# First transform of k times v crossed with the last quarter of the paired inverse; an arena part of its own, load tiles that share buffers

## The chip, the cores and the metric

The kernel runs on one core of one Trainium2 chip. The metric is device time in microseconds, from one launch of the program; every number called "us" is of that kind or a time inside one profiled execution. A difference between two kernels is given as a ratio of times.

A core has five engines with their own instruction streams. TensorE (PE) multiplies matrices and writes to PSUM, which has eight banks. ScalarE (ACT) and VectorE (DVE) read PSUM and SBUF. GpSimd (POOL) does little here. The sync engine (SP) issues nearly all DMA transfers, in one queue and in order. Engines wait for each other through semaphores.

## The reference

Inputs have S = 2048 rows and D = 1024 channels; the MLP has F = 3584. The kernel computes the output and the gradients of ten inputs (bf16).

```
xn   = layernorm(x)
ksh  = sum over t of shift(k, t) * shift_k[:, 3 - t]      # 4 taps along the sequence
kv   = ksh * v
y    = irfft(rfft(kv, 2S) * rfft(ssm_k, 2S))[:S] + kv * ssm_D
h    = relu(xn @ W_gate) * (xn @ W_up)
out  = x + xn * y + h @ W_down
```

The gradients with respect to x, k, v, shift_k, ssm_k, ssm_D, W_gate, W_up and W_down follow from it. For the long convolution that means three forward transforms per channel (ssm_k, the gated gradient g = grad_out * xn, and kv), products of spectra, and inverse transforms for y, for the gradient of ssm_k (gh) and for the gradient of kv (gkv).

## The kernel before

Two parts are woven together. `LnMlp` does layer norm and the MLP forward and backward: nearly all its work is 128x512 matmuls with a contraction over 128 rows, called big matmuls here. `ABranch` does the long convolution, in 8 groups of 128 channels, as small matmuls in corners of the array (32x64 or 64x32 pieces), evictions by ScalarE, transposes and products by VectorE.

`LnMlp` runs in phases. `hidden` makes gate, up and the gradient of h for a block of 512 columns of F at a time. For each row tile: 8 matmuls into ps_g, a ReLU on ScalarE (L1143), 8 into ps_u, a mask (L1150) and a product (L1156) on VectorE and a store; 8 into ps_h, an eviction on ScalarE (L1278), one product of the gradient with both halves of ru on VectorE (L1279) and a store of ug_d. The last rows of a block are marked `hold`. `grad_down` and `grad_in` make the gradients of the weights by `gemm16` and, at three places, by `four`, which keeps four accumulators, so four PSUM banks, at a time. `out_phase` and `grad_x` come last, after the branch has ended. I count big matmuls from the start of the program; `hidden` ends at 2765, and `four` covers 2765 to 2829 and 3597 to 3725.

The branch is a generator, `slots`: each item is one slot with a TensorE part (or None) and a VectorE part. `steps` (L575) takes the next slot when the MLP has issued enough matmuls: 1900 ns of them in the hidden phase, later 1900 after a slot with a TensorE part and 1250 after one without. A slot thus lies at a fixed place among the big matmuls. With `pri.strict` set, every engine keeps this program order.

Loads are queued by `fetch`. `steps` issues one queued load per slot, but none while `hold` is set; `need` issues what is queued up to a load that is about to be used. SP then takes them in its own order.

A group's steady course, with the names that the profile shows:

- The second forward transform of g and k·v (FW, `f2_pair`) reads two transposed tiles (`flp`) that VectorE made by `flip` (L332, two STREAM_TRANSPOSE for each tile).
- Spectral products on VectorE (`cmul`, `turn`: 128x2048 and 128x1024 tensor_tensor, recorded at L91).
- The first inverse of gkv (IA, `inv_a`), its first steps crossed with the next group's filter (`hn`); transposes; second inverse (RB, `inv_b`) with evictions at L87; gks and gv; their stores and the halo copies of gks.
- The paired first inverse of y and gh (`inv_a_pair`), four quarters of 32 matmuls each. Two are crossed with the first transform of the next group's g (`gt`), after `gate_grad` has multiplied gt by `xt`.
- The taps of the gradient of k (`tg`), flips, the y step (RB with a piece of the second filter transform), flips, the gh step.
- In between, the taps of the next group's k (`tk` into `ksh`), the product `kvt` = ksh * vt, its first transform (two steps of 8 matmuls, 512 columns wide), and flips of g and k·v for the next group.

All PSUM tiles, of both parts, come from one pool of eight banks. `crossed` (L495) takes two rounds each of an inverse and of a forward transform on different row quarters of the array and issues them alternately by `joint` as one step. Each of the four jobs of a forward round takes a bank, and so does each of an inverse's.

The tiles of the branch lie in pools: `lng` (ksh, kp, vt), `ld` (hn, gt), `a_xt` (xt), `ts` (three tiles for kvt, gks, gv, gk, yt, gh, gkv), and the arena of eight parts of 4096 columns, where the spectra and the row forms of g, k·v and the inverses (`Bg`, `Bk`, `Cs`, `Cy`, `Ch`) share parts. Part 6 holds `Bk` and also half of `Cs`, so the first transform of k·v cannot be written before the inverse's `Cs` has been transposed.

## Time and profile before

| what | us |
|---|---|
| median of 3 runs | 1860.21 (1859.41 to 1860.25) |
| profiled run | 1859.57 |
| span in it | 1857.8 |
| TensorE busy | 1836.3 (99%) |
| VectorE busy | 1114.7 (60%) |
| ScalarE busy | 646.0 (35%) |
| VectorE busy, 117 to 690 (branch and hidden phase) | 451.8 of 573 |
| VectorE busy, 690 to 1240 (branch and weight gradients) | 364.6 of 550 |

A line of a timeline gives start, duration, engine, line, operation, out<-in, tile and how many instructions were joined; in square brackets the idle time before it and what ended that. TensorE's granted clock is 1.000 throughout. Matmuls overlap: a big matmul lasts 0.38 us and the next begins 0.216 us after its start. The end of a matmul is modelled.

### The profile page before, as it was taken

Reading aid. Unit: us, or ns where it says so; the run is one execution under the profiler, and the core shown is the slowest. Engines: PE = TensorE matmul, PEld = TensorE weight load, DVE = VectorE, ACT = ScalarE, POOL = GpSimd, SP = SyncE. Lnnn points to the kernel's source line nnn. Section 1 sums busy time; section 2 is a strip of 40 time slices with the busy share of each in tenths; the row PEclk is TensorE's granted clock in tenths of the full one; section 3 lists DMA queues with packets and bytes.
Section 4 is the critical chain, followed back from the end, with each engine's and each line's share of the span. In section 5 each row is a group of like instructions: output and inputs, shape, how many; then the busy total and the mean of one; then the engine's idle time right before and its main releaser. Section 6 shows DMA issues by size and latency. Waiting matters only on the chain.

```text
span 1857.8 us, 31871 instructions
## 1 busy us (share of the span) xinstructions
PE 1836.3 (99%) x12840; PEld 844.2 (45%) x13061; DVE 1114.7 (60%) x1635; ACT 646.0 (35%) x1215; POOL 19.2 (1%) x51
## 2 busy tenths in 40 slices
PE   9999999999999999999999999999999999999999
PEld 4444444444444444444444444444444544444444
DVE  6656888798698777685585874801222222466652
ACT  5645444444545445544545454320000000111100
POOL 1000000000000000000000000000000000000000
PEclk9999999999999999999999999999999999999999
DMA  9898499779559838368474363488999857799973
GB/s 266 246 238 184 130 226 226 191 172 208 151 145 242 251 91 213 118 159 259 120 184 132 110 183 110 136 222 235 252 243 254 184 141 166 177 210 213 206 151 74
DMA packets 748132, 344.65 MB, mean 186 GB/s; under 512 B 576088, under 2 KB 715344, under 8 KB 747984
## 3 DMA queue, kind: packets, MB, share of 16 engines
q1 hardware_dynamic: 736848, 320.31, 71.2%
q10 hardware_dynamic: 9504, 17.04, 2.9%
q0 software_dynamic: 1632, 5.24, 0.8%
q8 instruction: 102, 1.67, 0.4%
q14 instruction: 46, 0.38, 0.1%
HBM read 143.79 MB, written 103.83 MB: 133 GB/s over the span
## 4 chain that ended last, share of the span: by engine, by line
PE 97%; issue 1%; DVE 1%; DMA 1%; ACT 0%; SPq 0%; DVEq 0%; ACTq 0%
PE ps_x L1666 21%; PE ps_w L1370 20%; PE ps_h L1035 10%; PE ps_g L1035 10%; PE ps_u L1035 10%; PE ps_o L1534 10%; PE ps_d L1370 9%; PE ps_c L83 4%; PE ps_d L1386 1%; PE ps_w L1386 1%; PE ps_r L1568 0%; DMA wu<-in_B_W_up_dram 0%; PE pst_x L1074 0%; DMA ugs<-ug_d 0%; DMA ln_x<-in_A_q_dram 0%
## 5 line engine op out<-in xcount | busy, mean ns | idle before, releaser
L1370 PE MATMUL ps_w<-ugs,xn_nat 128*128 128x512 bf16 x1673 | 376.0, 379 | 4.4 <-issue 2.4
L87 ACT CAST arena<-ps_c 128x512 bf16<-128x512 f32 x576 | 294.7, 609 | 76.5 <-PE ps_c L83 76.2
L1035 PEld LDWEIGHTS <-xnT 128*128 128x128 bf16 x1792 | 171.6, 98 | 210.7 <-issue 8.2
L332 DVE STREAM_TRANSPOSE arena<-arena 128x1024 f32<-128x1024 f32 x96 | 179.9, 1934 | 128.1 <-ACT arena L87 109.8
L1370 PEld LDWEIGHTS <-xn_nat 128*128 128x128 bf16 x1728 | 165.0, 98 | 201.8 <-issue 8.1
L1035 PE MATMUL ps_u<-wu,xnT 128*128 128x512 bf16 x873 | 205.0, 379 | 1.7 <-DMA wu<-in_B_W_up_dram 0.2
L1035 PE MATMUL ps_g<-wg,xnT 128*128 128x512 bf16 x871 | 204.4, 379 | 2.0 <-DVE xnT L1079 0.3
L1035 PE MATMUL ps_h<-wdT,goT 128*128 128x512 bf16 x867 | 203.0, 379 | 2.3 <-DVE ru L1150 0.7
L1666 PE MATMUL ps_x<-wgT,ggT 128*128 128x512 bf16 x879 | 197.5, 379 | 0.9
L1666 PE MATMUL ps_x<-wuT,guT 128*128 128x512 bf16 x877 | 197.4, 379 | 1.0
L1684 ACT ACTIVATE w<-xn,m 128x512 f32<-128x512 bf16 x32 | 24.3, 806 | 479.9 <-DVE m L1677 366.6
L1534 PE MATMUL ps_o<-wd,hT 128*128 128x512 bf16 (+1 forms) x878 | 186.6, 372 | 0.9
L1370 PE MATMUL ps_d<-g_nat,hs 128*128 128x512 bf16 x740 | 167.9, 379 | 1.9 <-issue 0.8
L1666 PEld LDWEIGHTS <-guT 128*128 128x128 bf16 x896 | 87.7, 98 | 105.7
L1666 PEld LDWEIGHTS <-ggT 128*128 128x128 bf16 x896 | 87.7, 98 | 105.5
L1278 ACT CAST gh<-ps_h 128x512 bf16<-128x512 f32 x112 | 66.4, 593 | 195.1 <-PE ps_h L1035 188.4
L1035 PEld LDWEIGHTS <-goT 128*128 128x128 bf16 x896 | 86.2, 98 | 104.3 <-issue 2.5
L1534 PEld LDWEIGHTS <-hT 128*128 128x128 bf16 x896 | 87.7, 98 | 99.9
L1373 ACT CAST wi<-ps_w 128x512 bf16<-128x512 f32 x108 | 64.4, 596 | 190.0 <-PE ps_w L1370 158.9
L1526 DVE TENSOR_TENSOR ya<-ya,xe 128x1024 bf16<-128x1024 bf16 x16 | 11.1, 693 | 185.0 <-DMA xe<-xn_d 185.0
L1150 DVE SCALAR_TENSOR_TENSOR ru<-ru,ps_u 128x512 bf16<-128x512 bf16 x112 | 76.4, 682 | 66.0 <-PE ps_u L1035 41.7
L91 DVE TENSOR_TENSOR t<-arena 128x2048 bf16<-128x2048 bf16 x96 | 113.8, 1219 | 0.5
(145 smaller groups left out, 1378.8 us busy)
## 6 DMA issues: line engine op xcount, KB each, us to landing
ugs<-ug_d SPq DMA_DIRECT2D x112, 256.0 KB
ug_d<-ru SPq DMA_DIRECT2D x110, 256.0 KB
wg<-in_B_W_gate_dram SPq DMA_DIRECT2D x56, 256.0 KB
wu<-in_B_W_up_dram SPq DMA_DIRECT2D x56, 256.0 KB
hs<-h_d SPq DMA_DIRECT2D x56, 256.0 KB
out_dram<-wi SPq DMA_DIRECT2D x56, 256.0 KB
h_d<-ht SPq DMA_DIRECT2D x108, 128.0 KB
gt<-in_grad_out_dram SPq DMA_DIRECT2D x32, 256.0 KB
```

Of the source, the lines that this page charges most:

```text
L83: self.pri.pin(self.nc.tensor.matmul(out, lhsT=lhsT, rhs=rhs, start=start, stop=stop))
L87: self.pri.pin(self.nc.scalar.copy(out=out, in_=in_))
L91: self.pri.pin(self.nc.vector.tensor_tensor(out=out, in0=in0, in1=in1, op=op))
L332: self.pri.pin(self.nc.vector.transpose(out=df[:, c0:c0 + 32, :], in_=sf[:, c0:c0 + 32, :]))
L1035: self.pri.pin(self.nc.tensor.matmul(ps[:], lhsT=xT[:, kt * P:(kt + 1) * P], rhs=w(kt), start=(kt == 0), stop=(kt == self.DT - 1)), always ...
L1150: return self.pri.pin(nc.vector.scalar_tensor_tensor(out=ru[s][:, 1, :], in0=ru[s][:, 0, :], scalar=0.0, in1=ps[:], op0=ALU.is_gt, op1=ALU ...
L1278: self.pri.pin(nc.scalar.copy(out=gh[:], in_=ps[:]))
L1370: self.pri.pin(self.nc.tensor.matmul(ps[:], lhsT=lhsT(st), rhs=rhs(st), start=(st == 0), stop=(st == self.ST - 1)))
L1373: self.pri.pin(self.nc.scalar.copy(out=out, in_=ps[:]))
L1386: self.pri.pin(self.nc.tensor.matmul(ps[i][:], lhsT=lhsT(i, st), rhs=rhs(i, st), start=(st == 0), stop=(st == self.ST - 1)))
L1534: nc.tensor.matmul(ps, lhsT=hT[:, kt, :], rhs=self.wd[:, kt, oc], start=(kt == 0), stop=(kt == self.FT - 1))
L1666: nc.tensor.matmul(ps, lhsT=T[:, kt, :], rhs=W[:, kt, oc], start=(i == 0), stop=(i == n - 1))
```

## The change

Crossing: `crossed` now takes the quarter's number k and returns just two steps. The paired inverse's quarter 0 is crossed with g as before, and its quarter 3 with the first transform of k·v of the next group. For this, `Bk` has its own ninth arena part, and ksh, kvt and the taps of the next group are made ahead of the end of the inverse, in the slots where gk's taps were; the gk taps move behind and round the crossing.

Buffers: hn and kp share one buffer (tag "hk"), xt and ksh share one ("kx"), the pool `a_xt` is gone, and kvt is written over kp. A load into a shared buffer waits for the last reader of the tile before. So xt is fetched after the stores of gv, just ahead of its use, k and its taps after the crossing with the filter, and the filter of the group after next after the k·v crossing.

Slots: the two flips of y, the y step, the two flips of h, the gh step, and the four flips of k·v and g follow each other without tap slots between. A steady group has 73 slots instead of 76, 16 with a TensorE part instead of 17. The first group is reordered likewise: the gate product in its first slot, then the filter and g, then k.

```diff
-        arena = self.pool("a_are", 1, side="right").tile([P, 8, NB1 * P], BF16, name="arena")
+        arena = self.pool("a_are", 1, side="right").tile([P, 9, NB1 * P], BF16, name="arena")
-        self.Bg, self.Bk, self.H, self.GKV = rows(7), rows(6), spectrum(4), spectrum(7)
+        self.Bg, self.Bk, self.H, self.GKV = rows(7), rows(8), spectrum(4), spectrum(7)
...
-        st["hn"] = self.ld.tile([P, 2, 32, NB1], BF16, name="hn")
+        hn = self.lng.tile([P, 19, P], BF16, name="hn", tag="hk")[:, 0:16, :].rearrange("p r c -> p (r c)")
...
-        xt = st["xt"] = self.xp.tile([P, 16, P], BF16, name="xt")
+        xt = st["xt"] = self.lng.tile([P, 16, P], BF16, name="xt", tag="kx")
...
-    def crossed(self, inv, fwd):
-        I, F = inv[0], fwd[0]
-        return [self.joint(I[0][0:1], I[1][0:1], F[2], F[3]), self.joint(F[0], F[1], I[2][0:1], I[3][0:1])] + inv[1][1:]
+    def crossed(self, I, F, k):
+        I = [g[k:k + 1] for g in I]
+        return [self.joint(I[0], I[1], F[2], F[3]), self.joint(F[0], F[1], I[2], I[3])]
...
     def start_kvt(self, st):
-        kvt = st["kvt"] = self.ttile("kvt")
-        self.tt(kvt[:, 0:16, :], st["ksh"][:], st["vt"][:], ALU.mult)
+        st["kvt"] = st["kp"][:, 0:16, :]
+        self.tt(st["kvt"], st["ksh"][:], st["vt"][:], ALU.mult)
...
         self.store_time(self.out_gv, st["cg"], gv)
+        self.fetch(nx, self.load_xn)
         yield [], lambda: self.halo(st)
-        self.fetch(nx, self.load_k, self.load_taps)
-        ia = self.inv_a_pair()
+        ia, inv = self.inv_a_pair()
+        q = self.cmul(K, G, True, G, 1)
+        yield inv[1], q
+        for _ in range(4):
+            yield None, q
+        q = self.cmul(H, K, False, K, 1)
         if last:
-            ia = [ia[1][0], None] + ia[1][1:]
+            cross = [inv[0], None]
         else:
             self.need(self.load_xn, nx)
             yield None, lambda: self.gate_grad(nx)
-            self.fetch(n2, self.load_xn)
-            ia = self.crossed(ia, self.fwd1(self.Bg, nx["gt"]))
...
+            cross = self.crossed(ia, self.fwd1(self.Bg, nx["gt"])[0], 0)
+        yield None, q
+        yield cross[0], q
         yield None, q
         yield None, q
...
+        yield cross[1], q
         self.fetch(n2, self.load_g)
+        f2H, cross = [], [inv[3], None]
+        if not last:
+            f2H = [(1, self.f2(H, 1, j)) for j in range(4)]
+            self.need(self.load_k, nx)
+            self.need(self.load_taps, nx)
+            self.begin(nx)
+            tk = nx["tk"]
+            yield None, tk
+            yield None, tk
+            yield inv[2], tk
+            yield None, tk
+            yield f2H[0:2], tk
+            yield None, tk
+            yield None, tk
+            self.need(self.load_v, nx)
+            yield None, lambda: self.start_kvt(nx)
+            cross = self.crossed(ia, self.fwd1(self.Bk, nx["kvt"])[0], 3)
...
+        yield cross[0], tg
         yield None, tg
         yield None, tg
...
+        yield cross[1], tg
+        self.fetch(n2, self.load_filter)
+        if not last:
+            yield None, tg
+            yield None, tg
         self.store_time(self.out_gk, st["cg"], gk)
         fly = self.flip_C(self.Cy, 0)
         yield None, fly
         yield None, fly
-        tk = None
-        if not last:
-            self.need(self.load_k, nx)
-            self.need(self.load_taps, nx)
-            self.begin(nx)
-            tk = nx["tk"]
-        yield None, tk
-        yield None, tk
-        yield f2H[2:3] + self.inv_b(st, "yt", 0), tk
+        yield f2H[2:3] + self.inv_b(st, "yt", 0), None
+        yield None, None
         self.store_time(self.y_d, st["cg"], st["yt"])
         flh = self.flip_C(self.Ch, 0)
         yield None, flh
         yield None, flh
-        yield None, tk
-        yield None, tk
-        yield f2H[3:4] + self.inv_b(st, "gh", 0), tk
-        yield None, tk
-        yield None, None
+        yield f2H[3:4] + self.inv_b(st, "gh", 0), None
...
-        yield None, lambda: self.start_kvt(nx)
-        f1k = self.fwd1(self.Bk, nx["kvt"])[1]
-        yield None, lambda: self.store_gh(st)
-        flG = self.flip_B(self.Bg, 0)
-        yield f1k[0], None
-        yield None, flG
-        yield f1k[1], flG
-        yield None, None
         flK = self.flip_B(self.Bk, 1)
         yield None, flK
         yield None, flK
+        flG = self.flip_B(self.Bg, 0)
+        yield None, self.both(lambda: self.store_gh(st), flG)
+        yield None, flG
         yield None, None
-        yield None, None
```

More of the change, by code (lines that the diff above doesn't have):

```diff
@@ L115, in open @@
         self.tmp = self.pool("a_tmp", 2, side=R)
-        self.xp = self.pool("a_xt", 1, side=R)
         self.sm = self.pool("a_sm", 2, side=R)
@@ L270, in load_filter @@
     def load_filter(self, st):
-        st["hn"] = self.ld.tile([P, 2, 32, NB1], BF16, name="hn")
+        hn = self.lng.tile([P, 19, P], BF16, name="hn", tag="hk")[:, 0:16, :].rearrange("p r c -> p (r c)")
+        st["hn"] = hn.rearrange("p (h c n) -> p h c n", h=2, n=NB1)
         self.load_rows(st, 0)
@@ L297, in load_k @@
         nc = self.nc
-        kp = st["kp"] = self.lng.tile([P, 19, P], BF16, name="kp")
+        kp = st["kp"] = self.lng.tile([P, 19, P], BF16, name="kp", tag="hk")
         self.pri.now()
@@ L588, in steps @@
         yield 3400
-        self.load_k(st)
-        self.load_taps(st)
-        yield 3400
         self.load_g(st)
@@ L594, in steps @@
         self.load_v(st)
+        yield 3400
+        self.load_taps(st)
         yield 6800
@@ L599, in steps @@
         self.open_arena()
-        self.begin(st)
         for st in self.sts:
@@ L613, in begin @@
     def begin(self, st):
-        st["ksh"] = self.lng.tile([P, 16, P], BF16, name="ksh")
+        st["ksh"] = self.lng.tile([P, 16, P], BF16, name="ksh", tag="kx")
         st["tk"] = self.taps(st, st["ksh"], st["kp"], [(3, 0), (2, 1), (1, 2), (0, 3)])
     def start_kvt(self, st):
-        kvt = st["kvt"] = self.ttile("kvt")
-        self.tt(kvt[:, 0:16, :], st["ksh"][:], st["vt"][:], ALU.mult)
+        st["kvt"] = st["kp"][:, 0:16, :]
+        self.tt(st["kvt"], st["ksh"][:], st["vt"][:], ALU.mult)
     def flip_H(self):
@@ L639, in first @@
     def first(self, st):
-        tk, f1h, nx = st["tk"], self.fwd1_filter(st)[1], self.ahead(st, 1)
-        yield f1h[0], None
-        yield None, tk
-        yield f1h[1], tk
-        self.fetch(nx, self.load_filter)
-        yield None, self.both(lambda: self.add_D(st), tk)
-        yield None, tk
+        f1h, nx = self.fwd1_filter(st)[1], self.ahead(st, 1)
+        yield f1h[0], lambda: self.gate_grad(st)
+        yield None, None
+        yield f1h[1], None
+        self.load_k(st)
+        f1g = self.fwd1(self.Bg, st["gt"])[1]
+        yield None, lambda: self.add_D(st)
         flH = self.flip_H()
+        yield f1g[0], flH
         yield None, flH
-        yield None, flH
-        yield None, tk
-        yield None, tk
-        f2H = [(1, self.f2(self.H, 1, j)) for j in range(4)]
-        yield f2H[0:2], lambda: self.gate_grad(st)
-        self.fetch(nx, self.load_xn)
-        yield None, tk
-        yield f2H[2:4], lambda: self.start_kvt(st)
-        yield None, None
-        f1g, f1k = self.fwd1(self.Bg, st["gt"])[1], self.fwd1(self.Bk, st["kvt"])[1]
-        yield f1g[0], None
-        yield None, None
         yield f1g[1], None
         self.fetch(nx, self.load_g)
+        f2H = [(1, self.f2(self.H, 1, j)) for j in range(4)]
+        yield None, None
+        flG = self.flip_B(self.Bg, 0)
+        yield f2H[0:2], flG
+        yield None, flG
+        self.begin(st)
+        tk = st["tk"]
+        yield None, tk
+        yield f2H[2:4], tk
+        for _ in range(5):
+            yield None, tk
+        yield None, lambda: self.start_kvt(st)
+        f1k = self.fwd1(self.Bk, st["kvt"])[1]
         yield None, None
         yield f1k[0], None
-        flG = self.flip_B(self.Bg, 0)
-        yield None, flG
-        yield f1k[1], flG
+        yield None, None
+        yield f1k[1], None
+        self.fetch(nx, self.load_filter)
         yield None, None
@@ L707, in slots @@
             self.need(self.load_rest, nx)
-            iaG = self.crossed(iaG, self.fwd1_filter(nx))
+            iaG = self.crossed(iaG[0], self.fwd1_filter(nx)[0], 0) + iaG[1][1:]
         yield iaG[0], q
@@ L713, in slots @@
         yield None, lambda: self.turn(H, 1, 1)
-        self.fetch(n2, self.load_filter)
+        self.fetch(nx, self.load_k, self.load_taps)
         q = self.cmul(K, G, True, G, 0)
@@ L750, in slots @@
             yield None, lambda: self.gate_grad(nx)
-            self.fetch(n2, self.load_xn)
-            ia = self.crossed(ia, self.fwd1(self.Bg, nx["gt"]))
-        yield None, None
-        q = self.cmul(K, G, True, G, 1)
-        yield ia[0], q
+            cross = self.crossed(ia, self.fwd1(self.Bg, nx["gt"])[0], 0)
+        yield None, q
+        yield cross[0], q
         yield None, q
         yield None, q
-        yield ia[1], q
-        yield None, q
-        q = self.cmul(H, K, False, K, 1)
+        yield cross[1], q
         self.fetch(n2, self.load_g)
-        yield None, q
-        yield ia[2], q
-        yield None, q
-        yield None, q
-        yield None, q
-        gk = self.ttile("gk")
-        tg = self.taps(st, gk, gks, [(0, 0), (1, 1), (2, 2), (3, 3)])
+        gk = self.ttile("gk") if last else None
+        tg = self.taps(st, gk, gks, self.TAPS) if last else None
+        f2H, cross = [], [inv[3], None]
[10 more added lines that the diff above has]
+            yield f2H[0:2], tk
+            yield None, tk
+            yield None, tk
+            self.need(self.load_v, nx)
+            yield None, lambda: self.start_kvt(nx)
+            cross = self.crossed(ia, self.fwd1(self.Bk, nx["kvt"])[0], 3)
+            gk = self.ttile("gk")
+            tg = self.taps(st, gk, gks, self.TAPS)
+        else:
+            yield inv[2], tg
+            yield None, tg
+        yield None, tg
+        yield cross[0], tg
         yield None, tg
         yield None, tg
-        yield ia[3], tg
-        yield None, tg
-        yield ia[4], tg
-        yield None, tg
-        f2H = [] if last else [(1, self.f2(H, 1, j)) for j in range(4)]
-        yield f2H[0:2], tg
+        yield cross[1], tg
+        self.fetch(n2, self.load_filter)
+        if not last:
+            yield None, tg
+            yield None, tg
         self.store_time(self.out_gk, st["cg"], gk)
@@ L780, in slots @@
         yield None, fly
-        tk = None
-        if not last:
-            self.need(self.load_k, nx)
-            self.need(self.load_taps, nx)
-            self.begin(nx)
-            tk = nx["tk"]
-        yield None, tk
-        yield None, tk
-        yield f2H[2:3] + self.inv_b(st, "yt", 0), tk
+        yield f2H[2:3] + self.inv_b(st, "yt", 0), None
+        yield None, None
         self.store_time(self.y_d, st["cg"], st["yt"])
@@ L793, in slots @@
         yield None, flh
-        yield None, tk
-        yield None, tk
-        yield f2H[3:4] + self.inv_b(st, "gh", 0), tk
-        yield None, tk
-        yield None, None
+        yield f2H[3:4] + self.inv_b(st, "gh", 0), None
         if last:
+            yield None, None
             yield None, lambda: self.store_gh(st)
             return
-        self.need(self.load_v, nx)
-        yield None, lambda: self.start_kvt(nx)
-        f1k = self.fwd1(self.Bk, nx["kvt"])[1]
-        yield None, lambda: self.store_gh(st)
-        flG = self.flip_B(self.Bg, 0)
-        yield f1k[0], None
-        yield None, flG
-        yield f1k[1], flG
-        yield None, None
         flK = self.flip_B(self.Bk, 1)
@@ L813, in slots @@
         yield None, flK
+        flG = self.flip_B(self.Bg, 0)
+        yield None, self.both(lambda: self.store_gh(st), flG)
+        yield None, flG
         yield None, None
-        yield None, None
+    TAPS = [(0, 0), (1, 1), (2, 2), (3, 3)]
 A_START = 60_000
```

## The prediction

> **What bounds the kernel now.** I read first the busy shares, then the chain of waits by engine, then the timelines of TensorE, VectorE, ScalarE and the sync engine's queue round the steps that move.

> ```profile
> PE 1836.3 (99%) x12840; PEld 844.2 (45%) x13061; DVE 1114.7 (60%) x1635; ACT 646.0 (35%) x1215; POOL 19.2 (1%) x51
> PE   9999999999999999999999999999999999999999
> DVE  6656888798698777685585874801222222466652
> PE 97%; issue 1%; DVE 1%; DMA 1%; ACT 0%; SPq 0%; DVEq 0%; ACTq 0%
> ```

> TensorE is the bound in all forty slices (granted clock 1.000). VectorE is at 0.8 to 0.9 in the first third, the hidden phase, where its queue also holds the MLP's masks and products. So the change can gain only TensorE time, and can lose whatever it makes TensorE wait.

> What a branch step costs TensorE, from its timeline:

> ```profile
> 1059.64 7.29 PE L1370 MATMUL ps_w<-ugs,xn_nat 128*128 128x512 bf16 x32
> 1066.86 0.30 PE L83 MATMUL ps_c<-arena,IA 32*64 32x256 bf16 x4
> ...
> 1067.43 3.63 PE L1370 MATMUL ps_w<-ugs,xn_nat 128*128 128x512 bf16 x15
> ...
> 1071.56 5.35 PE L1370 MATMUL ps_w<-ugs,xn_nat 128*128 128x512 bf16 x23
> 1076.84 0.64 PE L83 MATMUL ps_c<-arena,IA 32*64 32x256 bf16 x32
> 1077.42 2.76 PE L1370 MATMUL ps_w<-ugs,xn_nat 128*128 128x512 bf16 x12
> ...
> 1109.64 6.42 PE L1370 MATMUL ps_w<-ugs,xn_nat 128*128 128x512 bf16 x29
> 1115.99 0.42 PE L83 MATMUL ps_c<-kvt,R 32*64 32x512 bf16 x8
> 1116.35 3.63 PE L1370 MATMUL ps_w<-ugs,xn_nat 128*128 128x512 bf16 x15
> ```

> Big matmuls start 0.216 us apart and last 0.38, so a group's last start is its end less 0.38. Start to start over a step, less 0.22, is its price: g crossed with half an inverse round (1066.55 to 1067.43) 0.66; the full inverse quarter (1076.53 to 1077.42) 0.67; one k·v step (1115.68 to 1116.35) 0.45.

> The tail of a hidden group, VectorE then TensorE:

> ```profile
> 456.62 0.69 DVE L1279 TENSOR_TENSOR ru<-ru,gh 128x1024 bf16<-128x1024 bf16 x1 [1.02 <-ACT gh L1278]
> 457.22 3.71 DVE L332 STREAM_TRANSPOSE arena<-arena 128x1024 f32<-128x1024 f32 x2
> 460.78 1.21 DVE L91 TENSOR_TENSOR tap<-kp,skb 128x2048 bf16<-128x2048 bf16 x1
> 461.90 0.68 DVE L1150 SCALAR_TENSOR_TENSOR ru<-ru,ps_u 128x512 bf16<-128x512 bf16 x1
> 462.61 0.43 DVE L1156 TENSOR_TENSOR ht<-ru 128x512 bf16<-128x512 bf16 x1
> ```
> ```profile
> 458.04 3.62 PE L1035 MATMUL ps_u<-wu,xnT 128*128 128x512 bf16 x16
> 461.49 1.89 PE L1035 MATMUL ps_h<-wdT,goT 128*128 128x512 bf16 x8
> 463.31 0.25 PE L83 MATMUL ps_c<-arena,FW 64*32 64x128 bf16 x8
> ```

> The flips (transposes) end at 460.93, and the step that reads them starts at 463.31, 2.4 us later: two slots of taps lie between. Over the hidden phase this slack is 2.4 to 4.9 us, once 0.7. The sync queue round group 1's gate:

> ```profile
> 411.37 1.67 SPq L1053 DMA_TRANSPOSE wdT<-in_B_W_down_dram  x1
> 413.09 1.89 SPq L99 DMA_DIRECT2D vt<-in_A_v_dram  x2
> 415.08 0.77 SPq L1284 DMA_DIRECT2D ug_d<-ru  x1
> ...
> 420.71 2.26 SPq L99 DMA_DIRECT2D xt<-xn_d  x2
> ```

> **The change part by part.**

> *Crossing k·v with the inverse's last quarter.* Per group two k·v steps and one inverse quarter (2 x 0.45 + 0.67 = 1.57) become two crossed steps, taken at the price of the g crossing (2 x 0.66 = 1.32): 0.25 less, times 7 groups, 1.7 us. Other steps are cut differently (second-transform pieces that stood with the inverse or alone now stand elsewhere): 0.5 dearer by the same rows. Net **-1.2 us**. VectorE, ScalarE and DMA keep their amounts of work. The branch ends some 31 us earlier; nothing waits for it.

> *Taps no longer between the flips and their readers.* This is where I expect the loss. Flip, flip and the reading step are now in neighbouring slots, so what VectorE has before the flip decides. In the changed order, the last flip stands behind a mask and product, or behind a gradient product, whose own big matmuls end only eight matmuls ahead of the step. From the last of these matmuls' start: mask begins after 0.47 (the common value in the trace), then 0.68 + 0.03 + 0.42 - 0.08 + 1.93 (one flip) = 3.45 us. TensorE needs 8 x 0.216 plus 0.31 to enter the step, some 2.1. It waits **1.4**. Behind a gradient product: 0.42 to the eviction, 0.6 for it, 0.07, 0.69, less 0.08, 1.93 = 3.6: wait **1.5 to 1.6**. Two flips behind a gradient product sixteen matmuls ahead: 5.4 against 3.8: **1.6 to 1.7**. Read off place by place, hidden groups 0, 1, 2: yt step 1.4, 1.7, 1.6; gh step 1.6, 1.7, 1.4; the next group's second transform, which the k and g flips precede, 0.6, 0.75, 0.3. Sum **+11 us**. In the dense phase VectorE has no masks and slack is 3.2 to 7.2, of which two slots take 2.5: nothing, covered by what is left. If that cover went too, up to 1 us in each of 8 places.

> Two short waits of before (0.33 and 0.08, both on the mask after such a step) go: **-0.4**; late next is the step itself, as above.

> *PSUM in the stretches where four accumulators are held.* Two crossed k·v steps now fall into the second such stretch (after big matmuls 3618 and 3637). ScalarE's row after a crossing of before,

> ```profile
> 1067.32 3.03 ACT L87 CAST arena<-ps_c 128x512 bf16<-128x512 f32 x6 [1.49 <-PE ps_c L83]
> ```

> has six evictions, 0.5 each: a crossing writes six banks, and four of eight are held. The fifth tile must wait for the first eviction: 1.25 us after the step began against 0.2, then one more eviction, 0.45: 1.5; at the second 1.1; and two second-transform pieces that stand only two matmuls apart in the first stretch, 0.8. **+3.4 us**. Bounds: 0 (banks free in time) to 6 evictions x 0.5 x 2 = 6; I take the worked value. [...]

> *xt shares a buffer with ksh, so it is loaded late.* Before, xt was in 381 to 600 big matmuls ahead of the gate product (46 in the first group); now it is queued 0 to 18 ahead. From issue to landing an xt half took 4.2 to 6.6 us (issue against its semaphore), issue itself 0.65. In the hidden phase's held rows of group 1 no queued load is issued until its user asks, so in SP's order xt stands behind that wdT transpose, vt, ug_d: it would be issued near 416 on the scale of before, second half landing at 421 to 423, product (1.22) done by 422.5 to 424.5. The crossed step that reads it comes 16 matmuls behind the gate slot, near 415.5. Queued behind the gate on VectorE are the next masks, which release PSUM. TensorE waits 5 to 9, if SP runs somewhat ahead 5; I take **+7 us**. Other groups: xt is queued six slots ahead of the gate and the step comes two slots on. In a dense group gate end and step come out within 0.5 us of each other, so 0 to 2 us each; first group 0 to 1.8 (issue near 123 to 127, first step near 124, gate ahead of its taps). **+2 us** in all, bounds 0 and 14. [...]

> *hn and kp share, kvt in kp, ninth arena part.* In the changed order hn is loaded 75 or more big matmuls (16 us) ahead of use, kp 41 in the first group (9 us) and 155 or more after, vt 99 or more; landings took 3.8 to 8.4. Hidden; if one came late, a few us at most, once. kp's memset on POOL (1% busy) moves with its loads and waits for hn's last reader; a late load on SP delays only the stores and weight loads queued behind it. Bounds -0 and +4; I take 0.

> *Sum:* 1859.6 (profiled run; span 1857.8 in it; median of the runs 1860.2, 0.6 more) - 1.2 - 0.4 + 11 + 3.4 + 7 + 2 = 1881.4. **1881 us.**

> **The rivals.**

> 1. *Flips and banks cost, the loads are hidden* because SP runs ahead of the program's order: 1859.6 - 1.6 + 14.4 = 1872. For it: queues do run ahead. Against: ug_d before xt in SP's order waits for a gradient product of the same rows.
> 2. *Not slower:* the flips are done in time. The place is the chain mask, product, flip against eight matmuls; it decides at 2.1 us from the last matmul's start to the flip's end. Were VectorE to run a flip before those masks, all that remains is the saving: 1858 to 1860, the work on the banks and xt included only if hidden also. Against: each engine keeps program order, and 0.68 + 0.42 + 1.93 alone is 3.0.
> 3. *xt late in every group:* landing at 6.6 and a busy queue add 2 us in six groups where I took 2 in all: 1881 + 10 = 1891.
> 4. *The crossing doesn't save:* a k·v crossing at 0.67 + 0.45 loses 4.7 instead of winning 1.7 (2 x 1.12 against 1.57, seven times); within the range of all.

> **How the numbers follow.** Forecast 0.55 (own range 1874 to 1888), rival 1 0.2, rival 2 0.1, rival 3 0.15. A measurement of this kernel tells about 0.2%, 3.7 us, from no change. Faster by that needs more than the 1.2 saved and all waits of TensorE in this stretch (1.3 us) together, so 0.02; same 0.1; slower 0.88. The range 1866 to 1893 leaves out rival 2 and the far end of rival 3.

> **What the profile after would show.** k·v crossings as R rows among IA rows, 0.88 start to start, the lone kvt steps only in the first group: the saving is right. TensorE idle 1.4 to 1.7 before the FW/RB steps of the first three groups, released by VectorE's L332: flips right. VectorE idle on a DMA before gt<-gt,xt, and TensorE idle at the crossing after it: xt right. TensorE idle on ScalarE near the k·v crossings of the group that meets the held accumulators: banks right. What would make it wrong: transposes starting before the masks, loads issued well ahead, or a wait of the weight loads (wdT, wu) behind xt in SP's queue, which I have left at nothing because their tiles are fetched a block ahead.

## The result

The changed kernel takes 1902.85 us (5 runs, 1896.91 to 1903.00) against 1859.61 before (5 runs, 1859.41 to 1860.25). The ratio is 1.0223, interval 1.0208 to 1.0238. The profiled run took 1902.85, with a span of 1900.7. So the sign was right, but the loss of 43 us is twice the 21 that I forecast, and the time lies outside the range.

The page and the slices after:

```profile
span 1900.7 us, 31865 instructions
...
PE 1848.3 (97%) x12844; PEld 848.6 (45%) x13061; DVE 1115.8 (59%) x1635; ACT 647.4 (34%) x1215; POOL 19.2 (1%) x51
...
PE   9999999989899999998999999999999999999999
```

VectorE and ScalarE did the same work (1114.7 and 646.0 before). TensorE has fewer steps, yet its busy time grew by 12 us. That is the first sign of something that idle time alone does not explain. The waits of TensorE after (what it waited for, total, times, longest):

```profile
PE ps_c L83 <- DVE gt L91: 13.9, 3, 8.5
PE ps_c L83 <- DVE arena L332: 10.8, 9, 2.0
PE ps_w L1390 <- DMA xn_nat<-xn_d: 3.5, 7, 1.0
...
PE ps_c L83 <- ACT arena L87: 0.8, 2, 0.6
PE ps_c L83 <- DVE arena L91: 0.7, 2, 0.5
```

None of the five is among the waits before. The second line is the flips, nine waits in nine places as forecast, 10.8 us against 11. The first is xt, larger than forecast. The third is a load that I had put at nothing. The fourth is the banks. The fifth is one step of group 0 that waits twice for a spectral product; the forecast has no term for it. The timeline of TensorE round the gate of group 1:

```profile
420.15 0.30 PE L83 MATMUL ps_c<-arena,IA 32*64 32x256 bf16 x4
428.92 0.64 PE L83 MATMUL ps_c<-gt,R 32*64 32x512 bf16 x4 [8.47 <-DVE gt L91]
...
430.75 4.91 PE L1039 MATMUL ps_h<-wdT,goT 128*128 128x512 bf16 x14 [0.22 <-issue]
435.49 3.62 PE L1039 MATMUL ps_g<-wg,xnT 128*128 128x512 bf16 x16
```

After the wait, 14 big matmuls take 4.91 us where 16 take 3.62 a moment later. The granted clock says why (columns of a stretch: length, then busy time and instructions of each engine, then the clock, DMA share, GB/s):

```profile
420.00:424.00 4.00, 0.46 (x6) 0.11 (x4) 0.00 (x0) 0.00 (x0) 0.00 (x0) 1.00 1.31 203
424.00:428.00 4.00, 0.00 (x0) 0.00 (x0) 0.36 (x1) 0.00 (x0) 0.00 (x0) 0.50 0.84 117
428.00:434.00 6.00, 4.86 (x29) 1.86 (x31) 5.18 (x7) 3.49 (x7) 0.00 (x0) 0.50 0.14 45
434.00:440.00 6.00, 6.00 (x48) 2.67 (x48) 4.28 (x7) 2.17 (x5) 0.00 (x0) 0.98 0.51 134
```

The clock falls to a half in this wait, and TensorE pays for that after the wait is over. There are four such stretches in the profiled run: 423.98 to 434.22, 502.49 to 505.90, 895.02 to 898.43 and 1092.99 to 1099.82. The mean clock is 0.994; before, it was 1.000.

The loss adds up if it is counted from matmul start to matmul start, each interval against its usual value (884, 879, 1090 ns and so on over a step, 216 between big matmuls). Each trace lacks the records of some 220 of 8200 big matmuls; their places are taken from the weight loads, of which there is one for each. (Without these places xt comes to 16.3, the figure in an expectation below.)

| term | forecast | measured |
|---|---|---|
| crossing instead of separate steps, other steps cut differently | -1.2 | -1.3 |
| flips late for the y, gh and second-transform steps, less before's own such waits | +11 and -0.4 | +12.6 |
| xt late, g crossings (slow clock inside them included) | +9 | +15.7 |
| banks at the k·v crossings and one second-transform piece | +3.4 | +2.9 |
| xn_nat late | 0 | +4.7 |
| big matmuls at half clock | 0 | +7.6 |
| first inverse quarter of group 0, spectral product late | 0 | +1.0 |
| waits for wu that before had | 0 | -0.8 |
| sum | +21.8 | +42.4 |

The last big matmul starts 43.0 us later than before. The 0.6 left over was there ahead of the branch's first step, so it is no part of the change. Each wait weighs some 0.1 to 0.7 more in this count than in the view of waits, since a wait shows there only from the modelled end of the last matmul.

The second late xt, in group 6, shows where the dense phase failed. SP's timeline, then VectorE's, then TensorE's:

```profile
1074.92 4.49 SPq L1356 DMA_DIRECT2D ugs<-ug_d  x8
1079.64 0.36 SPq L107 DMA_DIRECT2D gks_d<-gks  x1
1080.43 2.07 SPq L107 DMA_DIRECT2D out_dram<-gv  x2
1082.55 4.36 SPq L99 DMA_DIRECT2D gks<-gks  x2
1086.96 0.59 SPq L99 DMA_DIRECT2D gks<-NX  x1
1087.59 1.39 SPq L99 DMA_DIRECT2D xt<-xn_d  x2
```
```profile
1082.12 1.28 DVE L91 TENSOR_TENSOR arena<-t 128x1024 bf16<-128x1024 bf16 x2
1093.07 1.23 DVE L91 TENSOR_TENSOR gt<-gt,xt 128x2048 bf16<-128x2048 bf16 x1 [9.66 <-DMA xt<-xn_d]
```
```profile
1088.94 0.30 PE L83 MATMUL ps_c<-arena,IA 32*64 32x256 bf16 x4
1094.35 0.64 PE L83 MATMUL ps_c<-gt,R 32*64 32x512 bf16 x4 [5.11 <-DVE gt L91]
...
1095.75 5.42 PE L1374 MATMUL ps_w<-ugs,xn_nat 128*128 128x512 bf16 x15 [0.33 <-issue]
```

xt stands behind the halo copies, and these behind the store of gks: in each group the first copy's issue ends within about 1 us of the landing of that store (1086.02 and 1086.15 here), as if it waited for it. VectorE had made gks by 1073.49, but vt and eight ugs loads came first and the store was issued at 1079.64, 6.1 us later. In group 5, where nothing but vt came first, it was 1.4 us later, and its crossing did not wait. The two halves of xt landed 4.0 and 4.7 us after their issue, about as traced before (4.2 to 6.6); it was the issue that came late.

### The profile page after: what moved, and what is told of

It reads as the page before. It is cut to its first block, busy times and chain, and to the rows that moved or that the text cites. A ratio compares the mean times of both kernels' runs of the same rounds, so it can differ in the third digit from the quotient of the medians.

```text
span 1900.7 us, 31865 instructions
## 1 busy us (share of the span) xinstructions
PE 1848.3 (97%) x12844; PEld 848.6 (45%) x13061; DVE 1115.8 (59%) x1635; ACT 647.4 (34%) x1215; POOL 19.2 (1%) x51
## 3 DMA queue, kind: packets, MB, share of 16 engines
q8 instruction: 102, 1.67, 0.4%
## 4 chain that ended last, share of the span: by engine, by line
PE 68%; DVE 2%; DMA 1%; issue 1%; SPq 1%; ACT 0%; DVEq 0%
PE ps_x L1670 20%; PE ps_w L1374 19%; PE ps_o L1538 10%; PE ps_d L1374 7%; PE ps_c L83 3%; PE ps_u L1039 2%; PE ps_g L1039 2%; PE ps_h L1039 2%; PE ps_d L1390 1%; DVE arena L332 1%; PE ps_w L1390 1%; SPq L99 1%; DMA xt<-xn_d 0%; PE ps_r L1572 0%; DMA xn_nat<-xn_d 0%
## 5 line engine op out<-in xcount | busy, mean ns | idle before, releaser
L87 ACT CAST arena<-ps_c 128x512 bf16<-128x512 f32 x576 | 294.0, 612 | 122.8 <-PE ps_c L83 122.6
L332 DVE STREAM_TRANSPOSE arena<-arena 128x1024 f32<-128x1024 f32 x96 | 179.8, 1930 | 106.2 <-ACT arena L87 75.6
L91 DVE TENSOR_TENSOR t<-arena 128x2048 bf16<-128x2048 bf16 x96 | 114.2, 1219 | 0.4
```

What stands on the lines that cost most here:

```text
L87: self.pri.pin(self.nc.scalar.copy(out=out, in_=in_))
L91: self.pri.pin(self.nc.vector.tensor_tensor(out=out, in0=in0, in1=in1, op=op))
L332: self.pri.pin(self.nc.vector.transpose(out=df[:, c0:c0 + 32, :], in_=sf[:, c0:c0 + 32, :]))
```

## The experiments

The theory: three places in the order (flips next to their readers, xt behind the halo, hn within the loads of xn_nat), and the clock as a surcharge on the waits. The rival: queue, VectorE or DMA engines are behind as a whole, and a wait taken away here comes back there.

**xt early.** The load of xt goes right after gv, which is the last reader of ksh:

```
         yield None, q
+        if not last:
+            self.load_xn(nx)
         self.store(self.gks_d[gi], ...)
...
-        self.fetch(nx, self.load_xn)
...
-            self.need(self.load_xn, nx)
```

> The changed kernel with one edit: xt of the next group is loaded as soon as gv, the last reader of ksh, is issued, ahead of the stores of gks and gv and of the halo copies. Theory (xt is late only because it is queued behind those): the waits of TensorE for the gate product (16.3 us counted start to start over the step, in groups 1 and 6) go, and with them the half-clock stretches after them, about 20 big matmuls at 0.216 more each, 4.3: 1903 - 20.6 = 1882. Rival (the queue and the DMA engines are behind altogether, an earlier place in the queue does not help, or the halo is late instead): 1895 or more, with the wait at the same crossings.

Measured: 1884.90 us (4 runs, 1882.46 to 1886.34), ratio 1.0129 (1.0114 to 1.0144); 18 us less. No wait for gt is left, and every g crossing but one takes 0.88 us (one reads 1.10, with a matmul record missing). The flips and banks stayed as they were (10.8 and 0.8). A part did come back elsewhere:

```profile
PE ps_c L83 <- DVE arena L332: 10.8, 9, 2.0
PE ps_w L1390 <- DMA xn_nat<-xn_d: 2.2, 5, 1.0
PE ps_u L1039 <- DMA wu<-in_B_W_up_dram: 2.0, 2, 1.5
```

wu stands behind the halo in SP's order, and the halo moved back by the time that xt took ahead of the gks store: its last copy was issued at 410.86, in the changed kernel at 408.17. The longer of its two waits, 1.5 us, was followed by a half-clock stretch (419.44 to 422.85). So the theory holds for xt, and the rival for some 2 us of it at most: the run with the filter later, which alters nothing near this place, also waited 1.4 for wu there, so part of it comes and goes by itself.

**Flips early.** In the hidden phase only, y's flips stand ahead of the last slot of gk's taps, h's ahead of the empty slot. The store of gk moved with it, in every group, to after y's flips:

```
         if not last:
             yield None, tg
-            yield None, tg
-        self.store_time(self.out_gk, st["cg"], gk)
         fly = self.flip_C(self.Cy, 0)
+        early = not last and not self.dense
+        if not early and not last:
+            yield None, tg
         yield None, fly
         yield None, fly
+        if early:
+            yield None, tg
+        self.store_time(self.out_gk, st["cg"], gk)
         yield f2H[2:3] + self.inv_b(st, "yt", 0), None
...
```

> The changed kernel with the order of VectorE's slots altered in the hidden phase alone: the flips of y one slot ahead (the last slot of gk's taps stands between them and the y step), the flips of h one slot ahead (the empty slot stands after them). TensorE's steps keep their places; the flips before the next group's second transform stay as they are. Theory (the flips' neighbourhood to their readers costs it): the six waits at the y and gh steps, 9.3 us together, go, the one of 2.1 us at the second transform and its half-clock stretch at about 502 stay: 1903 - 9.3 = 1893.5. Rival (VectorE as a whole is behind in the tail, the wait only moves to the next mask or the next flip): 1901 to 1904.

Measured: 1887.20 us (4 runs, 1886.34 to 1887.44), ratio 1.0142 (1.0127 to 1.0157); 15.7 less, more than the 9.3 expected. Of the six late y and gh steps two are left, with 0.45 and 0.87; start to start the six lost 8.5 us of their 9.8. Here is why it is more: this edit also put gk's store behind the last eight xn_nat loads, and that wait went altogether, 4.7 us and its stretch at half clock. And the wait of 2.0 at the second transform, though still there, fell so in time that no half-clock stretch followed. VectorE and TensorE in group 2, first of the changed kernel:

```profile
632.00 0.43 DVE L1160 TENSOR_TENSOR ht<-ru 128x512 bf16<-128x512 bf16 x1
632.35 1.95 DVE L332 STREAM_TRANSPOSE arena<-arena 128x1024 f32<-128x1024 f32 x1
634.14 0.67 DVE L1283 TENSOR_TENSOR ru<-ru,gh 128x1024 bf16<-128x1024 bf16 x1
634.73 1.90 DVE L332 STREAM_TRANSPOSE arena<-arena 128x1024 f32<-128x1024 f32 x1
```
```profile
634.64 0.38 PE L83 MATMUL ps_c<-arena,RB 64*32 64x512 bf16 x2
636.68 0.62 PE L83 MATMUL ps_c<-arena,RB 64*32 64x512 bf16 x14 [1.66 <-DVE arena L332]
```

The second flip stands behind a gradient product whose accumulator was ready only as the step drew near, and the rest of the step begins 0.05 us after the flip's end at 636.63. In the edited kernel both flips are through one slot earlier, and the step runs without a wait from 628.46:

```profile
621.09 1.95 DVE L332 STREAM_TRANSPOSE arena<-arena 128x1024 f32<-128x1024 f32 x1
...
626.24 1.94 DVE L332 STREAM_TRANSPOSE arena<-arena 128x1024 f32<-128x1024 f32 x1
628.03 0.66 DVE L1290 TENSOR_TENSOR ru<-ru,gh 128x1024 bf16<-128x1024 bf16 x1
628.63 1.19 DVE L91 TENSOR_TENSOR gk<-gk,tap 128x2048 bf16<-128x2048 bf16 x1
```

That VectorE is behind as a whole is refuted: the same work in another order takes the waits away.

**The filter later.** Where four accumulators are held, the filter is fetched after the gh step:

```
-        self.fetch(n2, self.load_filter)
+        wait = self.cap == 2
+        if not wait:
+            self.fetch(n2, self.load_filter)
...
+        if wait:
+            self.fetch(n2, self.load_filter)
         flK = self.flip_B(self.Bk, 1)
```

> The changed kernel with one edit: where four accumulators are held at the k times v crossing (one group), the filter of the group after next is fetched after the gh step instead of right after that crossing. Theory (the sixteen loads of xn_nat were late because hn, which waits in the sync queue, stood in their middle): the seven waits for xn_nat, 3.5 us, and the half-clock stretch near 895, 1.7 us, go: 1903 - 5.2 = 1897.7. Rival (the DMA engines are full there, 0.97 to 1.15 of share, and the loads are late wherever hn stands): 1902 to 1904 with the waits still there.

Measured: 1895.26 us (4 runs, 1892.78 to 1896.58), ratio 1.0182 (1.0165 to 1.0199); 7.6 less. No wait for xn_nat is left and no half clock near 895; a wait of 1.4 for wu at 416 is new, but lies far ahead of the place where this edit acts. SP's queue in the changed kernel shows what was in the way:

```profile
870.83 4.33 SPq L1069 DMA_DIRECT2D xn_nat<-xn_d  x5
875.72 5.55 SPq L99 DMA_DIRECT2D hn<-in_A_ssm_k_dram  x4
881.36 2.07 SPq L107 DMA_DIRECT2D out_dram<-gk  x2
883.53 5.89 SPq L1069 DMA_DIRECT2D xn_nat<-xn_d  x8
```

Between the eighth and the ninth load of xn_nat lie hn and gk's store, 7.8 us of SP's time; the last eight were issued from 883.53 on, and the first wait for one of them ended at 889.43. Full DMA engines (a share of 0.98 from 888 to 891 and 1.04 from 891 to 895 in the changed kernel) were not the cause: the order alone made the loads punctual. In this run and in the one before, one of the two that stood in the middle was moved, and either was enough.

**Matmuls that fill the wait.** 34 and 18 idle matmuls (128x512) ahead of the g crossings of groups 1 and 6; they compute nothing that is used.

```
+            if gi in self.FILL:
+                cross[0] = self.filled(cross[0], self.FILL[gi])
...
+    FILL = {1: 34, 6: 18}
+
+    def filled(self, step, n):
+        def go():
+            t = self.bank("ps_f")
+            for _ in range(n):
+                self.mm(t[:], self.identA[:], self.FW[:].rearrange("p l r c -> p (l r c)")[:, 0:512])
+            step()
+        return go
```

> The changed kernel with matmuls that do nothing useful (128x512, into a bank of their own) ahead of the g crossing in group 1 (34) and group 6 (18), to keep TensorE busy while xt is late: 7.3 and 3.9 us of work in waits of 8.5 and 5.1. Theory (a stretch of 3.41 us in which TensorE is busy half or less makes the next one run at half clock): no half clock after these two crossings, which cost 2.65 and 2.7 us: 1903 - 5.3 = 1897.5, clock 0.997 to 0.998. Rival (the clock falls for another reason, such as the load of the matmuls that follow): no gain, 1903, or up to 3 us more where the fillers outlast the wait.

Measured: 1895.05 us (4 runs, 1894.47 to 1896.25), ratio 1.0186 (1.0171 to 1.0201), mean clock 0.999. More work on TensorE made the kernel 7.8 us faster. In group 1:

```profile
419.35 7.50 PE L83 MATMUL ps_f<-FW,ident 128*128 128x512 bf16 x34
426.78 0.30 PE L83 MATMUL ps_c<-arena,IA 32*64 32x256 bf16 x4
428.15 0.41 PE L83 MATMUL ps_c<-gt,R 32*64 32x512 bf16 x4 [1.07 <-DVE gt L91]
...
428.75 3.61 PE L1051 MATMUL ps_h<-wdT,goT 128*128 128x512 bf16 x16
```

xt came no earlier; the crossing had its gt at 428.15 instead of 428.92, on a time scale that differs by some 0.7 already, and 16 matmuls then took 3.61. In group 6 a rest of 2.0 us remained, and the clock still fell for one stretch of 3.41. That the gain is above the 5.3 expected has a cause that the edit did not set: the stretches near 500 and 895 are absent here as well, although their waits are there (10.8 for the flips, 2.4 for xn_nat). How a wait lay to the stretches decided here, by the counts in the last section.

**All three repaired.** The three edits together, one empty slot more in each hidden group ahead of the next second transform, k·v uncrossed in the one group that meets the held accumulators, and xt at a better place:

```
         self.store(self.gks_d[gi], ...)
+        if not last:
+            self.load_xn(nx)
         yield None, q
         self.store_time(self.out_gv, st["cg"], gv)
...
+            one, f1k = self.cap == 2, self.fwd1(self.Bk, nx["kvt"])
+            cross = [f1k[1][0], f1k[1][1]] if one else self.crossed(ia, f1k[0], 3)
...
+        if one:
+            yield None, None
+            yield inv[3], None
```

> The changed kernel with the three edits together (flips early in the hidden phase, and one empty slot more there before the next group's second transform; the filter later where four accumulators are held; xt early), with two differences: xt is loaded between the store of gks and that of gv, where the halo copies wait for the store's landing anyway, since in the run with xt ahead of both stores TensorE waited 2.0 us for wu, which stands behind the halo; and in the one group that meets the four held accumulators k times v is not crossed but has two steps of its own. Theory (the crossing saves what the rows say, and all else of the loss was places): some 1.5 us of flips left, banks and loads nothing, saving 1.2 to 1.5: 1859.5 to 1861, the same as before within 0.2%, clock 0.999 or 1.000. Rival (the crossing or the ninth arena part costs something that no wait shows): 1864 or more.

Measured: 1865.34 us (6 runs, 1863.13 to 1869.56), ratio 1.0029 (1.0018 to 1.0041); the profiled run took 1863.13. It lies above the 1859.5 to 1861 expected, though the clock is 1.000 throughout. In the profiled run 1.5 us of wu in group 1 are left,

```profile
PE ps_u L1056 <- DMA wu<-in_B_W_up_dram: 1.5, 1, 1.5
...
PE ps_c L83 <- DVE arena L332: 0.9, 2, 0.4
PE ps_c L83 <- DVE arena L91: 0.8, 2, 0.5
```

and start to start some 1.5 at three y and gh steps, 1.0 at two second transforms and 1.0 at group 0's first inverse quarter. The other runs were up to 6 us longer than the profiled one, and no trace shows what they waited for.

**Uncrossed.** The repaired kernel with two k·v steps and a separate last quarter in every group:

```
-            one, f1k = self.cap == 2, self.fwd1(self.Bk, nx["kvt"])
+            one, f1k = True, self.fwd1(self.Bk, nx["kvt"])
```

> The repaired kernel with k times v not crossed in any group: two steps of its own and the last inverse quarter by itself, as before the change; all buffers and orders else stay. By the rows each group then costs 0.25 us more, six groups 1.5: 1861 to 1862.5, and the steps that read kp are 0.66 start to start and alone. Rival (the crossed step costs as much as the two it replaces): no difference, or faster than the repaired kernel.

Measured: 1864.58 us (8 runs, 1863.90 to 1867.52), ratio 1.0025 (1.0015 to 1.0036). Between the two profiled runs there are 1.5 us, as the rows say (1863.13 and 1864.61); between the medians there are -0.8. The comparison is inconclusive: 1.5 us is 0.08%, and the waits that moved with the slots outweigh it. The rows themselves are plain: a crossed k·v step 0.88 start to start, a single one 0.66, a full quarter 0.88.

**Two slots more.** The repaired kernel with one more empty slot ahead of the y and of the gh step in the hidden phase:

```
         if early:
             yield None, tg
+            yield None, None
         self.store_time(self.out_gk, st["cg"], gk)
...
         if early:
             yield None, None
+            yield None, None
```

> The repaired kernel with two empty slots more per group in the hidden phase, one ahead of the y step and one ahead of the gh step (the branch has some 80 us to spare at its end). What was left in the repaired kernel's profiled run: 1.5 us for wu in group 1, about 1.5 at the y and gh steps and 1.2 at the second transform. Theory (all of it is order: with another slot the flips end ahead, and wu's loads come in the queue before the store of gks and its halo): some 3 us less than the repaired kernel's 1863 to 1865, so 1859.5 to 1862, within 0.2% of before, and not beyond it, as the crossing is worth 1.5 at most. Rival (something the waits of TensorE do not show): 1863 to 1866 again.

Measured: 1859.09 us (11 runs, 1858.51 to 1859.48) against 1859.97 (15 runs, 1858.91 to 1861.61), ratio 0.9994 (0.9985 to 1.0003). The waits that are left:

```profile
PE ps_u L1058 <- DMA wu<-in_B_W_up_dram: 0.9, 2, 0.7
PE ps_c L83 <- DVE arena L91: 0.7, 2, 0.5
...
PE ps_c L83 <- DVE arena L332: 0.3, 1, 0.3
```

So the whole loss of 43 us was order, the one crossing at held banks included, which this kernel leaves uncrossed. With the order repaired, the crossing brings at most what the rows promised, which a measurement here cannot tell from nothing. Part of it is taken back by the wait for the spectral product in group 0 (L91), which stands in every version after the change and in none of the runs is moved.

## Why the prediction was wrong

*What bounds the kernel, and the ceiling of the gain:* right. TensorE bounds it, the crossing is worth 1.2 to 1.7 us, and no version was measurably faster than before.

*The crossing's price:* right; 12 of the 14 crossed k·v steps took 0.88, as the g crossing did, and the other two are the ones with held banks.

*The flips:* right in mechanism, in the places and in the total. Nine waits, 10.8 us in the view of waits, 11 forecast; the edit that undoes the neighbourhood took most of the y and gh waits away. That the total fits so well is partly luck: the six waits at the y and gh steps, 9.4 by the forecast, are 7.2 in that view, and the three at the second transform, 1.7 by the forecast, are 3.6. One of these, 2.0 where I had 0.75, brought a half-clock stretch. The two waits of before that I read as 0.33 and 0.08 are 0.66 and 0.20 in its timeline.

*The banks:* right: 2.4 us at the two crossings and 0.5 at the second-transform piece, against 3.4. TensorE waited there for ScalarE's evictions, where the crossing asks for six banks:

```profile
867.86 0.41 PE L83 MATMUL ps_c<-kp,R 32*64 32x512 bf16 x4
867.98 0.39 PE L83 MATMUL ps_c<-arena,IA 32*64 32x256 bf16 x8
868.94 0.89 PE L83 MATMUL ps_c<-kp,R 32*64 32x512 bf16 x4 [0.57 <-ACT arena L87]
```

*xt, group 1:* the mechanism was right, the size at the top of its bounds. Forecast 5 to 9, taken 7; 8.5 in the view of waits and 9.2 start to start. SP did not run ahead of the order: it issued xt at 420.37, on a time scale that was 4.5 us later than before's, and I had written 416 on that one.

*xt, the other groups: this step failed.* "In a dense group gate end and step come out within 0.5 us of each other, so 0 to 2 us each" took the issue of xt from the mean course of the queue. It holds for five of the six, but in group 6 ugs loads pushed the store of gks back, the halo followed its landing, and the cost was 5.8 us. I should have added up SP's queue for each group from the loads ahead, as I did for group 1.

*hn: this step failed.* "Hidden; if one came late, a few us at most, once", with 0 taken. I had asked whether hn itself would be punctual, which it was, and not who stands behind it in SP's queue; the forecast says itself that a late load delays what is queued behind it, and prices that at nothing. It was issued into the middle of sixteen xn_nat loads: 4.7 us and a stretch at half clock.

*The clock was missing from the sum.* Each wait was priced at its own length. This term failed by being left out: the half-clock stretches that four of the places brought cost 7.6 us on big matmuls, and some more inside steps. They are 3.41, 6.83 and 10.24 us long in the changed kernel, and TensorE was busy for 0.00 to 0.40 of the 3.41 us ahead of each fall (last section). Before's clock was 1.000 throughout, so no trace that the forecast was read from has a number for this. After the wait of 8.5 us in group 1, 14 big matmuls took 4.91 us where 16 take 3.62: the 7 us of the forecast stood for 7 and some more.

*A wait in group 0 was missing too.* In the changed order the first inverse quarter follows the halo copies directly. TensorE waits there for 0.45 and 0.28 us, at 250.98 and 251.57, for a product that VectorE wrote at 250.24 to 251.53, among the MLP's masks; start to start that is 1.0 us, most of what the crossing saves.

Of the 21.1 us that the sum lacked (42.9 by the spans against 21.8), 6.7 are xt, 4.7 xn_nat, 7.6 the clock, 2.0 the flips and 1.0 the product; the banks and wu came out somewhat below the forecast. The rivals did not hold: SP did not hide the loads (it did stand ahead of VectorE at times: in the trace of before it waited 49 times for ht to be written, 94.4 us in all), VectorE did not run the flips ahead of masks, xt was not late in every group but much in two, and a crossed k·v step cost 0.66 net and not 1.12.

## What to carry to other kernels

A step that is moved takes its transfers with it: for each, write down what stands behind it in its queue, and who waits for that, before asking whether the transfer itself is in time. Waits of TensorE can cost more than their length: in the changed kernel one of 2.0 us and a row of seven of up to 1.0 us (the xn_nat loads) each brought 3.41 us at half clock, and those of 8.5 and 5.1 us for xt brought 10.24 and 6.83; what of these lay behind the wait was paid on top of it. And a change that saves 0.25 us on a step should leave the neighbourhood of all other steps alone: seven such savings were lost 25 times over in the slots that moved with it, and repairing the order gave back no more than the start.
